# Attention of chunk 3 in 64x64 quarters, narrower P V products in chunks 3 to 7, and the next chunk's transposes moved between the two parts of attention

## The chip, the cores and the metric

One NeuronCore of a Trainium2 chip runs the kernel. The metric is the device time of one execution in microseconds (us); a kernel is run several times and the median is taken. Beside the times there is a profile of one execution. Its engines are PE (TensorE matmuls), PEld (TensorE weight loads), DVE (VectorE), ACT (ScalarE), POOL (GpSimd) and SP (SyncE, here only the queue that issues most of the DMAs). In the profile's shapes, "64*128 64x256" is a matmul with 64 rows and 128 columns of weights whose moving operand has 256 columns. One fp32 matmul instruction of the kernel shows as two matmul records and two weight loads.

## The reference, cut to what matters

The first half is an mLSTM cell over 4 batches, 8 heads, 768 steps and 40 dimensions, the second half a feed-forward layer on its output.

```python
for t in range(S):
    m_new = np.maximum(f_gate[:, :, t] + m, i_gate[:, :, t])
    f_stab = np.exp(f_gate[:, :, t] + m - m_new)
    i_stab = np.exp(i_gate[:, :, t] - m_new)
    m = m_new
    C = f_stab * C + i_stab * einsum('bhd,bhe->bhde', vt, kt)
    n = f_stab * n + i_stab * kt
    h_tilde = einsum('bhde,bhe->bhd', C, qt)
    denom = maximum(abs(sum(n * qt)), 1.0)
    y[:, :, t] = sigmoid(o_gate) * h_tilde / denom
x = y.transpose(0, 2, 1, 3).reshape(3072, 320)
out = maximum(x @ w_in, 0) ** 2 @ w_out      # w_in 320 x 2048, w_out 2048 x 320
```

## The kernel before

**Chunks.** The sequence is cut into chunks of 128 tokens, six per batch, 24 in all, numbered s. Inside a chunk the recurrence is written as attention. With k and q of a chunk transposed (`transposes`, PE, followed by two copies out of PSUM), `scores` forms k q for all pairs of tokens, `weigh` makes the decay weights W (ACT), `mask` and `mask_W` set the pairs to zero in which the key is later than the query token (POOL), and `weighted` multiplies scores by W into P (DVE). P has keys in rows and tokens in columns, so its block of late keys (64 to 127) and early tokens (0 to 63) is all zero. The output of a chunk is P V plus the state C of the chunk before times q; the new state is a decayed C plus k V.

**Three ways of attention.** Chunks 0 to 3 use `attend`: full-height matmuls, `hi` (C q, 4 instructions with 82 columns), `dC` (k V, 4 with 82) and `hp` (P V, 8 with 41). Chunks from `X_SQ` = 4 on use `attend_begin` and `attend_end`: 64x64 quarters of the array, so that four matmuls of different quarters can run beside each other, with the output turned (`numT`). Two quarters that add into the same place of PSUM may not do so at once, so the work is in two parts, with the rows swapped in the second, and between the parts stands a small DVE instruction (L718, one element) that reads the last output of the first part and writes a spare element of kq which the second part reads. In chunks 4 to 7 `values_of_P` (L746) multiplies all 128 columns of P in both parts. In chunks from `ROT` = 8 on the zero block is left out already (the second part has 64 columns).

**Order of the work.** The order on each engine is that in which the code issues it; it is written by hand. The first phase is the loop over u = 0 to 7, where s = 2 + u // 2. In an even u come the scores of chunk s and a part of the first product of the feed-forward layer (`ffn1`); in an odd u come the attention of chunk s, the transposes of chunk s + 1 (L553), the copies out of PSUM (L556, ACT), and another part of `ffn1` (L896 and L907). Between them runs the rounding of the weights (`rounding`): ACT takes the raw words apart (L216, L218), three DVE instructions follow (L227, L231, L232), and POOL joins the result into `w_in` or `w_out` (L236). Each `ffn1` part waits for the pieces of `w_in` that it reads. In u = 3 the attention of chunk 3 stands in the DVE queue behind the rounding of the last pieces of `w_in`.

The second phase starts at chunk 6. `ffn2` (L934) gives the first two chunks' rows of the output; from n = 4 on `ffn1_open` and `ffn1_close` (L1056) and `ffn2_fast` (L980) do the feed-forward layer with fewer products, made from sums of blocks: `sums_of_x` (L1048, L1051, DVE for the first group) needs the normalised rows of chunks 4 and 5, transposed. These rows go through memory: the output of a chunk is stored by SP (`store_num`, L795), loaded turned (`load_num`, L800), normalised on DVE (`normalise_turned`, L812 to L825), stored (`store_rows`, L850), loaded again (`load_rows`, L855) and transposed on DVE in squares (`turn_squares`, L862). SP issues these in program order, each after the landing of the one that it depends on. The first `ffn1_open` multiplies a block X from xT and then a block Y from the sum at L1051.

The state of chunks 1 to 5 is in two tiles `C_old` (by head pairs, two halves) whose flat views are `C_flat`. `decay_old` (POOL) makes the decayed state Cd for the next chunk.

Of the kernel before, what the change touches and what calls it, by code (L numbers as in the profile page):

```python
# [9 lines left out]
F32 = mybir.dt.float32  # L10
# [4 lines left out]
ALU = mybir.AluOpType  # L15
PSUM = bass.MemoryType.PSUM

P = 128
# [11 lines left out]
def kernel(  # L30
# [27 lines left out]
    nc = tc.nc  # L58
    B, H, S, D = q.shape
    BH = B * H  # L60
    NB = S // P
    NT = B * NB
    PR = H // 2
    DP = 64
    D1 = D + 1
# [6 lines left out]
    W = 4 * P  # L72
# [10 lines left out]
    ps_at = ctx.enter_context(tc.tile_pool(name="ps_at", bufs=3, space=PSUM))  # L83
# [236 lines left out]
    st = {}  # L320
# [11 lines left out]


    SQ = 32
    KQ_SQ, X_SQ, ROT = 7, 4, 8
    HALVES = slice(0, DP), slice(DP, 2 * DP)

    def pair_up(s):
# [48 lines left out]
    def kqT(s):  # L387
        t = kqT_b[s % NKT]
        st.setdefault(s, {}).update(kT=t[:, 0], qT=t[:, 1])
        return t  # L390
# [156 lines left out]
    def transposes(s, o=(False, False)):  # L547
        d = st[s]
        kqT(s)
        for i, n in enumerate(("kT", "qT")):  # L550
            tp = bank(o[i])
            for j in range(PR):
                nc.tensor.transpose(  # L553
                    tp[:, j, :], d["kq"][:, i, 2 * j : 2 * j + 2, :].rearrange("p h d -> p (h d)"), ident[:],
                )
            (nc.vector.tensor_copy if s == 1 else nc.scalar.copy)(d[n], tp)  # L556

    def scores(s, o=(False, False)):
        d = st[s]
# [41 lines left out]
            nc.vector.tensor_tensor(t, d["sc"][i], d["W"][:, heads, :] if s < ROT else t, op=ALU.mult)  # L601

    C_old, C_flat = [], []

    def num_tile():
        return old.tile([P, 4 * P], F32, name="num", bufs=1)

    def decay_old(s):
        if s + 1 < NB:
            Cd = st[s]["Cd"] = old.tile([P, PR, 2, D1], F32, name="Cd", bufs=1)  # L610
            if s >= X_SQ:
                st[s]["Cd"] = Cd = Cd[:].rearrange("p j i d -> p (j i d)")[:, : PR * D1].rearrange("p (j d) -> p j d", d=D1)
                for i, rows in enumerate(HALVES):
                    nc.gpsimd.tensor_tensor(
                        Cd[rows], C_old[(s - 1) % 2][rows, :, i, :],
                        st[s]["dec"][rows, i::2].unsqueeze(2).to_broadcast([DP, PR, D1]), op=ALU.mult,
                    )
                return
            nc.gpsimd.tensor_tensor(
                Cd[:].rearrange("p j i d -> p (j i) d"), C_old[(s - 1) % 2].rearrange("p j i d -> p (j i) d"),  # L620
                st[s]["dec"][:].unsqueeze(2).to_broadcast([P, H, D1]), op=ALU.mult,
            )

    def attend(s):
# [48 lines left out]
        if c + 1 < NB:  # L673
# [7 lines left out]
            if s != 1:  # L681
                decay_old(s + 1)

    def scale_q(s):
        if s % NB > 0:
            d = st[s]
            nc.vector.tensor_tensor(d["eA"], d["eA"], d["qT"], op=ALU.mult)

    def decay_C(s):
        if s % NB > 0:  # L690
# [2 lines left out]
                Cd, C_b[(s - 1) % 2][:, : PR * D1].rearrange("p (j d) -> p j d", d=D1),  # L693
                st[s]["eA"][:, :, P - 1 : P].to_broadcast([P, PR, D1]), op=ALU.mult,
            )

    LIVE = [slice(DP * i, DP * i + D) for i in range(2)]

    def state(s):
        return (C_b if s >= NB else C_flat)[s % 2]  # L700
# [1 line left out]
    def attend_begin(s):  # L702

        b, c = divmod(s, NB)
        d = st[s]
        out = d["out"] = [ps_at.tile([P, W], F32, name="numT", tag="at") for _ in range(2)]
        d["numT"] = [t[:, : 2 * P].rearrange("p (c t) -> p c t", t=P) for t in out]
        d["dC"] = [t[:, 2 * P : 2 * P + 2 * D1].rearrange("p (e d) -> p e d", d=D1) for t in out]
        if c > 0:
            values_of_C(s, (0, 1))  # L710
        for i in range(2):
            values_of_P(s, i, (0, 1), False)
        if c + 1 < NB:
            new_C(s, (0, 1), False)
            end, spare = out[1][DP : DP + 1, 2 * P + D1 : 2 * P + D1 + 1], d["kq"][DP : DP + 1, 0, 2, DP - 1 :]
        else:
            end, spare = out[1][DP : DP + 1, P : P + 1], state(s - 1)[0:1, 4 * D1 : 4 * D1 + 1]
        nc.vector.tensor_scalar(spare, end, scalar1=0.0, scalar2=None, op0=ALU.mult)  # L718

    def values_of_C(s, rows, order=(0, 1)):  # L720
        d = st[s]
        C = state(s - 1)
        for e in order:
            for m in order:
                i, j = rows[m], 2 * m + e
                at = (2 * j + i if s == X_SQ else j) * D1
                nc.tensor.matmul(  # L727
                    d["numT"][m][HALVES[e], i, :], lhsT=C[LIVE[i], at : at + DP], rhs=d["eA"][LIVE[i], j, :],
                    start=(i == m), stop=False, skip_group_check=True,
                )  # L730
# [5 lines left out]
    def values_of_P(s, i, rows, second):  # L736
        d = st[s]
        t0 = DP if second and s >= ROT else 0
        for e in range(2):
            for m in range(2):  # L740
                at, keys = slot(s, m, e, i, second), HALVES[rows[m]]
                if s < ROT:
                    rhs = d["P"][i][keys, 2 * m + e, :]
                else:
                    rhs = d["P"][i][keys, e, slice(0, DP) if second else slice(DP, 3 * DP)]
                nc.tensor.matmul(  # L746
                    d["numT"][m][HALVES[e], i, t0:], lhsT=va_w[s % NKQ][keys, at * D1 : at * D1 + DP], rhs=rhs,
                    start=(s % NB == 0 and i == 0 and not second), stop=True, skip_group_check=True,
                )
# [44 lines left out]
    def store_num(s):  # L794
        nc.sync.dma_start(n_d[s], st[s]["tn"].rearrange("p m j r -> p (m j r)"))  # L795
# [31 lines left out]
    def normalise(s):  # L827
        d = st[s]
        num = d["num"]
        if num is not d["hp"]:  # L830
            nc.vector.tensor_tensor(num, num, d["hp"][:], op=ALU.add)
        dm = work.tile([P, H], F32, name="dm")
        nc.vector.tensor_scalar(dm[:], num[:, :, D], scalar1=-2.0, scalar2=2.0, op0=ALU.mult, op1=ALU.max)
        nc.vector.scalar_tensor_tensor(dm[:], in0=num[:, :, D], scalar=2.0, in1=dm[:], op0=ALU.mult, op1=ALU.max)
        nc.vector.reciprocal(dm[:], dm[:])

        x = d["x"] = work.tile([P, 3 * P], F32, name="x_sb")
        x3 = x[:, :DM].rearrange("p (h d) -> p h d", d=D)
        nc.vector.scalar_tensor_tensor(x3, in0=d["og"], scalar=1.0, in1=num[:, :, :D], op0=ALU.add, op1=ALU.mult)
        nc.vector.tensor_tensor(x3, x3, dm[:].unsqueeze(2).to_broadcast([P, H, D]), op=ALU.mult)  # L840
# [323 lines left out]
    load_part(2, 0)  # L1164
    load_part(2, 1)
    idle(12)
    transposes(0)
    idle(4)
    spread_mask(0)
    spread_mask(0)  # L1170
# [9 lines left out]
    eA_turned = turn_gates(A_sb, eA_T, later=True)  # L1180
    weigh(0)
    eA_turned()
    transposes(1, (False, True))
    scores(0)
    spread_mask(1)
    spread_mask(1)
# [28 lines left out]
    turn_rows(0)  # L1215
    idle(2)
    turn_rows(1)
    transposes(2)
    weigh(2, masked=True)
    decay_old(2)  # L1220
    rounding.words()
# [5 lines left out]
    for u in range(8):  # L1227
        s = 2 + u // 2
# [38 lines left out]
        else:  # L1267
# [7 lines left out]
            if u == 5:  # L1275
                half_tanh(4)
                half_tanh(5)
            if s < X_SQ:
                attend(s)
            else:  # L1280
                attend_begin(s)
                attend_end(s)
                store_num(s)
            if u == 3:
                square_half()
            if u != 3:
# [11 lines left out]
                load_A(7)  # L1298
            if u > 4:
                load_num(s)  # L1300
            transposes(s + 1, (True, True))
            rounding.words()
            ffn1(u // 4, u % 4)
            if u != 3:
# [212 lines left out]
```

## Time and profile before

| | |
|---|---|
| median of 3 runs | 486.27 us (486.13 to 487.68) |
| span of the profiled execution | 485.6 us |
| PE busy | 476.8 us (98%), 6229 matmul records and as many weight loads |
| DVE, ACT, POOL busy | 341.1, 243.3, 228.2 us |
| granted TensorE clock | 1.000 over the span |
| DMA share, 50 to 86 us and 132 to 300 us | 0.98 and 0.75 |

The profiled execution's own time is known as its span; what lies around it is inside the 0.7 us by which the median stands above it. PE is busy all the time, so what matters is the time in which PE does nothing or does work that isn't needed, and what PE would wait for if it came earlier. The first phase ends near 86 us and has the densest DMA traffic; from 132 us on the pattern repeats with a period of about 37 us.

### The profile page before, as it was taken

What the parts mean: (1) busy time and instruction counts of PE and PEld (TensorE: products, weight loads), DVE (VectorE), ACT (ScalarE), POOL (GpSimd) and SP (SyncE); (2) the same over time, 40 slices, a digit from 0 to 9 for tenths busy, and PEclk for the clock granted to TensorE, in tenths of its full rate; (3) what the DMA queues carried; (4) which work ended last, traced back from release to release, by engine and by line L of the source; (5) the groups of instructions that cost most, each with busy time, mean ns of one, the idle gap of its engine ahead of it and who ended that gap; (6) DMA issues with size and microseconds to landing.
All of it is one profiled execution on the core that took longest, in us unless ns stands there. A gap on an engine that the chain in (4) does not pass through costs nothing.

```text
span 485.6 us, 15406 instructions
## 1 busy us (share of the span) xinstructions
PE 476.8 (98%) x6229; PEld 445.3 (92%) x6229; DVE 341.1 (70%) x719; ACT 243.3 (50%) x534; POOL 228.2 (47%) x335
## 2 busy tenths in 40 slices
PE   8999999999999999999999999998999999999997
PEld 5886887779999999999999999998999999999997
DVE  7879778788986766767776866765966956635441
ACT  4699797635733722923723932732942741513300
POOL 5464554657598196098097097098084040020000
PEclk9999999999999999999999999999999999999999
DMA  8999997789977767778867757758645613210000
GB/s 181 225 246 266 262 222 206 206 139 205 176 157 192 130 122 205 134 140 185 141 130 195 136 118 203 139 114 208 125 98 155 126 45 84 52 33 2 1 28 27
DMA packets 192695, 69.92 MB, mean 144 GB/s; under 512 B 158128, under 2 KB 181360, under 8 KB 192624
## 3 DMA queue, kind: packets, MB, share of 16 engines
q1 hardware_dynamic: 186400, 58.68, 56.3%
q0 software_dynamic: 6080, 10.16, 9.0%
q8 instruction: 49, 0.80, 0.7%
q14 instruction: 22, 0.18, 0.2%
q10 hardware_dynamic: 144, 0.10, 0.1%
HBM read 55.69 MB, written 18.92 MB: 154 GB/s over the span
## 4 chain that ended last, share of the span: by engine, by line
PE 87%; DVE 6%; ACT 3%; issue 2%; POOL 1%; DMA 1%; DVEq 0%; POOLq 0%
PE h_ps L980 34%; PE h_ps L1056 24%; PE h_ps L1089 6%; PE h_ps L896 4%; PE h_ps L934 4%; PE numT L746 3%; PE numT L727 2%; PE numT L757 1%; PE h_ps L907 1%; PE h_ps L579 1%; PE tp L587 1%; PE tp L553 1%; PE tp L579 1%; PE hp L660 1%; DMA i_sb<-in_i_gate_dram 1%
## 5 line engine op out<-in xcount | busy, mean ns | idle before, releaser
L478 POOL TENSOR_SCALAR_AFFINE_SELECT A_bc<-A_bc 64x512 f32<-64x512 f32 x32 | 24.3, 759 | 88.1 <-ACT kq L496 56.2
L1070 ACT COPY r_sb<-h_ps 128x512 f32<-128x512 f32 x20 | 11.7, 586 | 84.6 <-PE h_ps L1056 84.6
L980 PE MATMUL h_ps<-T,S 128*128 128x160 f32 x352 | 51.7, 300 | 0.5 <-ACT g L1105 0.5
L980 PEld LDWEIGHTS h_ps<-T,S 128*128 128x128 f32 x352 | 48.9, 190 | 1.0 <-ACT g L1105 0.9
L980 PE MATMUL h_ps<-w_out,g 128*128 128x160 f32 x336 | 49.2, 303 | 0.0
L980 PEld LDWEIGHTS h_ps<-w_out,g 128*128 128x128 f32 x336 | 46.1, 190 | 1.3 <-issue 0.7
L996 DVE TENSOR_TENSOR y_sb<-y_sb,h_ps 128x160 f32<-128x160 f32 x44 | 14.0, 319 | 45.6 <-PE h_ps L980 45.4
L1056 PE MATMUL h_ps<-xT,w_in 128*128 128x128 f32 x320 | 43.2, 278 | 0.6 <-issue 0.6
L1056 PE MATMUL h_ps<-lent_t,w_in 128*128 128x128 f32 x320 | 42.3, 275 | 0.0
L1056 PEld LDWEIGHTS h_ps<-xT,w_in 128*128 128x128 f32 x320 | 39.2, 192 | 2.0 <-issue 1.7
L375 POOL DMA_DIRECT2D va<-in_v_dram x64 | 39.2, 623 | 3.0 <-DMA kq_rows<-in_k_dram 2.5
L1089 PE MATMUL h_ps<-xT,w_in 64*64 64x128 f32 x960 | 39.1, 272 | 0.0
L1056 PE MATMUL h_ps<-lent_t 128*128 128x128 f32 x320 | 39.0, 275 | 0.0
L1056 PEld LDWEIGHTS h_ps<-lent_t,w_in 128*128 128x128 f32 x320 | 38.9, 192 | 0.0
L1056 PEld LDWEIGHTS h_ps<-lent_t 128*128 128x128 f32 x320 | 37.3, 192 | 0.0
L509 ACT ACTIVATE A_bc<-A_bc,b_R 128x64 f32<-128x64 f32 (+1 forms) x128 | 35.7, 361 | 2.3 <-POOL A_bc L478 1.9
L1089 PEld LDWEIGHTS h_ps<-xT,w_in 64*64 64x64 f32 x960 | 34.8, 133 | 1.3
L780 DVE STREAM_TRANSPOSE tn<-numT 128x256 f32<-128x256 f32 x36 | 14.1, 428 | 29.1 <-PE numT L727 20.0
L896 PE MATMUL h_ps<-xT,w_in 128*128 128x256 f32 x128 | 29.8, 383 | 0.5 <-POOL w_in L236 0.4
L1048 POOL TENSOR_TENSOR lent_t<-xT 128x128 f32<-128x128 f32 (+1 forms) x18 | 14.6, 829 | 32.7 <-DVE xT L862 32.7
L980 PE MATMUL h_ps<-w_out,g_c 128*128 128x160 f32 x192 | 28.0, 302 | 0.0
L896 PEld LDWEIGHTS h_ps<-xT,w_in 128*128 128x128 f32 x128 | 23.5, 190 | 4.5 <-POOL w_in L236 1.3
(223 smaller groups left out, 1150.1 us busy)
## 6 DMA issues: line engine op xcount, KB each, us to landing
A_bc<-a_slots SPq DMA_DIRECT2D x32, 256.0 KB, 4.5
kq<-num_rows SPq DMA_DIRECT2D x80, 64.0 KB, 2.4
num_rows<-tn SPq DMA_DIRECT2D x18, 256.0 KB, 2.6
raw<-in_moe_w_out_dram SPq DMA_DIRECT2D x7, 640.0 KB, 5.8
kqT<-kq_rows SPq DMA_DIRECT2D x34, 128.0 KB, 3.8
og<-in_o_gate_dram SPq DMA_DIRECT2D x24, 160.0 KB, 5.1
x_rows<-x_sb SPq DMA_DIRECT2D x20, 192.0 KB, 3.6
xT<-x_rows SPq DMA_DIRECT2D x80, 48.0 KB, 3.4
```

The source lines that it names most:

```text
L375: eng.dma_start(dst[HALVES[n], PR * (1 - late_keys) : PR * (2 - late_keys)], src[HALVES[late_keys], PR * m : PR * (m + 1)],)
L478: nc.gpsimd.affine_select(part, part, compare_op=ALU.is_ge, fill=-1e30, base=0, pattern=[[0, PR], [0, 2], [1, DP]], channel_multiplier=-1,)
L509: nc.scalar.activation(A[0][:, x, to], A[0][:, x, to], AF.Exp, bias=b_R[:, b, c, own, x : x + 1],)
L746: nc.tensor.matmul(d["numT"][m][HALVES[e], i, t0:], lhsT=va_w[s % NKQ][keys, at * D1 : at * D1 + DP], rhs=rhs, start=(s % NB == 0 and i == ...
L780: nc.vector.transpose(to[:, 2 * m : 2 * m + 2], d["numT"][m].rearrange("p c t -> p (c t)"))
L896: nc.tensor.matmul(hs[i][:, n, :], lhsT=w_in[:, a, fb * P : (fb + 1) * P], rhs=xT[:, :, a, :], start=(n == 0 and a == 0), stop=False,)
L934: nc.tensor.matmul(st["o_ps"][j], lhsT=st["g2", 0][:, fb, j * P : (j + 1) * P], rhs=w_out[:, fb, :], start=(fb == 0), stop=(fb == NF - 1),)
L980: nc.tensor.matmul(to, lhsT=lhsT[:, p], rhs=rhs[:, p, :], start=(start and p == 0), stop=(p == NPAIR - 1), skip_group_check=True,)
L996: add = lambda to, a, b: nc.vector.tensor_tensor(to, a, b, op=ALU.add)
L1048: sub = lambda to, a, b: eng.tensor_tensor(to, a, b, op=ALU.subtract)
L1056: nc.tensor.matmul(to[:, n, :], lhsT=lhsT[:, 4 * q + n, :], rhs=rhs, start=(start and n == 0), stop=True, skip_group_check=True,)
L1089: nc.tensor.matmul(to[cols, n, :], lhsT=w_in2[rows, 4 * q + n, cols], rhs=rhs, start=(start and n == 0), stop=True, skip_group_check=True,)
```

## The change

Chunk 3 gets an attention of its own in 64x64 quarters (`QUART` = 3): `rows_begin` with 16 instructions for C q, 12 for P V and 8 for k V, each with 41 columns, and `rows_end` with 8 for k V and 12 for P V. It has two parts and a one-element DVE instruction between them, as the later chunks have. The output isn't turned; DVE takes it in two halves. The four blocks of P V per head pair are three, the zero block is not multiplied. The state of chunk 3 is written flat, so chunk 4 reads it flat; Cd of chunk 3 is made by two POOL instructions on 64 partitions in place of one on 128. In chunks 4 to 7 those matmuls of `values_of_P` that read late keys take 64 columns in place of 128. In u = 3, 5 and 7 `transposes(s + 1)` is issued between the two parts of attention, and its copies out of PSUM are issued where they were.

```diff
     SQ = 32
-    KQ_SQ, X_SQ, ROT = 7, 4, 8
+    QUART, KQ_SQ, X_SQ, ROT = 3, 7, 4, 8
...
     def transposes(s, o=(False, False)):
...
-            (nc.vector.tensor_copy if s == 1 else nc.scalar.copy)(d[n], tp)
+            made.append((d[n], tp))
+
+        def copies():
+            for to, tp in made:
+                (nc.vector.tensor_copy if s == 1 else nc.scalar.copy)(to, tp)
+
+        return copies
...
     def decay_old(s):
-            if s >= X_SQ:
+            if s >= QUART:
...
                 for i, rows in enumerate(HALVES):
+                    C = C_old[(s - 1) % 2][rows, :, i, :]
+                    if s > QUART:
+                        C = C_flat[(s - 1) % 2][rows, : PR * D1].rearrange("p (j d) -> p j d", d=D1)
                     nc.gpsimd.tensor_tensor(
-                        Cd[rows], C_old[(s - 1) % 2][rows, :, i, :],
+                        Cd[rows], C,
...
+    def quarter(s, i, half, at, lhsT, rhs):
+        d = st[s]
+        nc.tensor.matmul(
+            d["out"][i][HALVES[half], at : at + D1], lhsT=lhsT, rhs=rhs, start=(i, half) not in d["begun"], stop=True,
+            skip_group_check=True,
+        )
+        d["begun"].add((i, half))
+
+    def rows_of_P(s, swap):
+        for j in range(PR):
+            for keys, toks in ((0, 0), (1, 1), (0, 1)):
+                i = keys ^ swap
+                quarter(
+                    s, i, toks, j * D1, d["P"][i][HALVES[keys], j, HALVES[toks]], d["va"][HALVES[keys], 2 * j + i, :],
+                )
+
+    def rows_of_k(s, swap):
+        for e in (1, 0) if swap else (0, 1):
+            for i in range(2):
+                for m in range(2):
+                    keys, h = HALVES[m ^ swap], 4 * m + 2 * e + i
+                    quarter(s, m, i, 2 * HD + e * D1, d["kq"][keys, 0, h, :], d["vw"][keys, h, :])
+
+    def rows_begin(s):
+        for j in range(PR):
+            for toks in range(2):
+                for i in range(2):
+                    quarter(
+                        s, i, toks, HD + j * D1, d["qT"][LIVE[i], j, HALVES[toks]],
+                        C_old[(s - 1) % 2][LIVE[i], j, i, :],
+                    )
+        rows_of_P(s, 0)
+        rows_of_k(s, 0)
+        end, spare = d["out"][1][DP : DP + 1, 2 * HD + D1 : 2 * HD + D1 + 1], d["kq"][DP : DP + 1, 0, 2, DP - 1 :]
+        nc.vector.tensor_scalar(spare, end, scalar1=0.0, scalar2=None, op0=ALU.mult)
+
+    def rows_end(s):
+        rows_of_k(s, 1)
+        rows_of_P(s, 1)
+        num = d["num"] = num_tile()[:, : H * D1].rearrange("p (h d) -> p h d", d=D1)
+        for i in range(2):
+            nc.vector.tensor_tensor(
+                num[:, i::2, :], view(d["out"][i], HD), eA_T[:, b, c, i::2].unsqueeze(2).to_broadcast([P, PR, D1]),
+                op=ALU.mult,
+            )
+        Cn = C_flat[s % 2][:, :HD].rearrange("p (m x) -> p m x", m=2)
+        for m in range(2):
+            nc.vector.tensor_tensor(
+                Cn[:, m], d["out"][m][:, 2 * HD : 2 * HD + 2 * D1],
+                d["Cd"].rearrange("p (m e) d -> p m (e d)", m=2)[:, m], op=ALU.add,
+            )
+        decay_old(s + 1)
...
     def values_of_P(s, i, rows, second):
                 if s < ROT:
-                    rhs = d["P"][i][keys, 2 * m + e, :]
+                    t0 = DP * rows[m]
+                    rhs = d["P"][i][keys, 2 * m + e, t0:]
...
     def normalise(s):
-        if num is not d["hp"]:
+        if s == QUART:
+            for i in range(2):
+                nc.vector.tensor_tensor(num[:, i::2, :], num[:, i::2, :], d["hp"][i], op=ALU.add)
+        elif num is not d["hp"]:
...
-            if s < X_SQ:
+            if s < QUART:
                 attend(s)
             else:
-                attend_begin(s)
-                attend_end(s)
-                store_num(s)
+                (rows_begin if s < X_SQ else attend_begin)(s)
+                copies = transposes(s + 1, (True, True))
+                (rows_end if s < X_SQ else attend_end)(s)
+                if s >= X_SQ:
+                    store_num(s)
...
-            transposes(s + 1, (True, True))
+            if s < QUART:
+                copies = transposes(s + 1, (True, True))
+            copies()
             rounding.words()
             ffn1(u // 4, u % 4)
```

More of the change, by code (lines that the diff above doesn't have):

```diff
@@ L549, in transposes @@
         kqT(s)
+        made = []
         for i, n in enumerate(("kT", "qT")):
@@ L603 @@
     C_old, C_flat = [], []
+    LIVE = [slice(DP * i, DP * i + D) for i in range(2)]
     def num_tile():
@@ L682, in attend @@
                 decay_old(s + 1)
+    HD = PR * D1
+    def quarter(s, i, half, at, lhsT, rhs):
[6 more added lines that the diff above has]
+    def rows_of_P(s, swap):
+        d = st[s]
+        for j in range(PR):
[4 more added lines that the diff above has]
+                )
@@ new lines, in rows_of_k @@
+    def rows_of_k(s, swap):
+        d = st[s]
+        for e in (1, 0) if swap else (0, 1):
[4 more added lines that the diff above has]
+    def rows_begin(s):
+        d = st[s]
+        d["out"], d["begun"] = [ps_at.tile([P, W], F32, name="numT", tag="at") for _ in range(2)], set()
+        for j in range(PR):
[9 more added lines that the diff above has]
+        nc.vector.tensor_scalar(spare, end, scalar1=0.0, scalar2=None, op0=ALU.mult)
@@ new lines, in rows_end @@
+    def rows_end(s):
+        b, c = divmod(s, NB)
+        d = st[s]
+        rows_of_k(s, 1)
+        rows_of_P(s, 1)
+        view = lambda t, at: t[:, at : at + HD].rearrange("p (j d) -> p j d", d=D1)
+        num = d["num"] = num_tile()[:, : H * D1].rearrange("p (h d) -> p h d", d=D1)
+        d["hp"] = [view(t, 0) for t in d["out"]]
+        for i in range(2):
[10 more added lines that the diff above has]
+        decay_old(s + 1)
@@ L695, in decay_C @@
             )
-    LIVE = [slice(DP * i, DP * i + D) for i in range(2)]
     def state(s):
@@ L725, in values_of_C @@
                 i, j = rows[m], 2 * m + e
-                at = (2 * j + i if s == X_SQ else j) * D1
+                at = j * D1
                 nc.tensor.matmul(
@@ L1166 @@
     idle(12)
-    transposes(0)
+    transposes(0)()
     idle(4)
@@ L1182 @@
     eA_turned()
-    transposes(1, (False, True))
+    transposes(1, (False, True))()
     scores(0)
@@ L1217 @@
     turn_rows(1)
-    transposes(2)
+    transposes(2)()
     weigh(2, masked=True)
```

## The prediction

> **What bounds the kernel now.** I read the page first, then the chain that ended last, then the order in time of each engine around chunks 3 to 7, and at last SP's queue. From the page, the busy times, the shares of the chain and the queue that carries PE's instructions:
>
> ```profile
> PE 476.8 (98%) x6229; PEld 445.3 (92%) x6229; DVE 341.1 (70%) x719; ACT 243.3 (50%) x534; POOL 228.2 (47%) x335
> ...
> PE 87%; DVE 6%; ACT 3%; issue 2%; POOL 1%; DMA 1%; DVEq 0%; POOLq 0%
> ...
> q8 instruction: 49, 0.80, 0.7%
> ```
>
> PE is busy 98% and carries 87% of the chain, so PE work taken out is worth its time if nothing else comes late. PE's order in time around chunks 3 and 4 (start, length, instruction; idle time before it in brackets):
>
> ```profile
> 47.99 1.12 PE L637 MATMUL hi<-Co,kqT 128*128 128x82 f32 x8
> 48.94 1.06 PE L649 MATMUL dC<-vw,kq 128*128 128x82 f32 x8
> 49.84 1.92 PE L660 MATMUL hp<-va,g_c 128*128 128x41 f32 x16
> 51.58 1.07 PE L553 MATMUL tp<-ident,kq 128*128 128x128 f32 x8
> 52.49 3.62 PE L896 MATMUL h_ps<-xT,w_in 128*128 128x256 f32 x16
> ...
> 64.35 0.39 PE L757 MATMUL numT<-vw,kq 64*64 64x41 f32 x16
> 65.02 0.44 PE L757 MATMUL numT<-vw,kq 64*64 64x41 f32 x16 [0.28 <-DVE kq L718]
> 65.28 0.65 PE L746 MATMUL numT<-g_c,va 64*64 64x128 f32 x16
> 65.74 0.40 PE L727 MATMUL numT<-kq,Co 40*64 40x128 f32 x8
> 66.08 1.09 PE L553 MATMUL tp<-ident,kq 128*128 128x128 f32 x8
> ```
>
> Start to start, full-height matmuls of 41 columns (L660) cost 109 ns a record (1.74 us for 16), quarters of 41 columns (L757) 13 to 16 ns (0.26 us for 16). Between the parts of chunk 4 PE waits for the DVE instruction L718. At the same time on DVE and POOL:
>
> ```profile
> 49.64 0.69 DVE L232 SCALAR_TENSOR_TENSOR mag<-raw,mag 128x512 int32<-128x512 int32 x1
> 50.25 0.49 DVE L668 TENSOR_TENSOR num<-hi,eA_T 128x328 f32<-128x328 f32 x1
> 50.48 1.27 POOL L236 TENSOR_TENSOR w_in<-mag,low 128x512 int32<-128x512 int32 x1 [1.16 <-DVE mag L232]
> ```
>
> DVE reaches the attention of chunk 3 at 50.25 only, and the last piece of `w_in` is done at 51.75. Both follow from a DVE queue without a gap since 40.57, which no PE work of this change feeds.
>
> **Chunk 3.** Old: 47.99 to 51.58, 3.59 us. New: 36 instructions, 72 records, before the wait, 20 instructions, 40 records, after it. At 58 ns a round of four (0.20 to 0.26 us for L757's four rounds), with C q in 8 rounds, P V in 8 (three of four quarters used) and k V in 4, the first part takes 1.16 us; the second, 4 and 8 rounds, 0.70. That is 1.73 us of PE work less. The Trainium skill speaks against it: "TensorEngine Tiling (Array Packing)", section "Instruction Overhead", gives each matmul some 60 cycles and advises against tiling a dimension that is small already; at the 25 ns which that estimate makes, 112 records are 2.8 us and 0.8 us less. L757's 13 to 16 ns with 41 columns say otherwise.
>
> Not all of it counts. The first part ends near 49.2, the transposes (0.91 us) near 50.2 with 0.1 us for the change of form on each side (L727 to L553: 0.34 us where its 8 records take 0.22). The one-element instruction takes 0.16 us on DVE and starts at 50.25, behind L232, so PE goes on at 50.46 and ends the second part near 51.25, against 52.49 for the same place. Then `ffn1` issues one matmul and its second waits for POOL's 51.75. Such a wait stands in the trace at 43.70, 0.05 us after the L236 that ends at 43.65, with L907 3.22 us later. So L907 starts at 51.80 + 3.22 = 55.02 against 56.04: **1.02 us** earlier. Without POOL's wait it would be about 1.2. Transposes of chunk 4 need its k and q, issued by SP at 37.94 and 38.38 and landed by 46.2, early enough.
>
> On DVE one short instruction comes new and num, the state and the sum are two halves each (L668's 0.49 becomes two of some 0.3): x of chunk 3 ends near 55.2, not 54.66, while PE reads it near 56.1. The cover is 0.9 us; beyond it the delay would be PE's. POOL's Cd of chunk 3 is two instructions (1.39 us for two such at 53.60, 0.74 for the one at 35.7), in 1.1 us in which POOL is idle. It may hold DVE's L231 beside it 0.3 us longer or let it go 0.3 earlier; I take 0.
>
> **Chunks 4 and 5.** Between the parts PE starts 0.50 us after its last start where a round takes 0.06: 0.45 us lost at 65.02, as much at 78.39. The transposes fill it, and have two changes of form more, 0.1 us each: **0.25 us** each, 0.5 together (0 if the changes cost 0.2, 0.45 if nothing). DVE is idle before L718 there, and the copies out of PSUM stay behind other ACT work.
>
> **The zero blocks.** L746 takes 0.44 us for 16 records, four rounds of 109 ns. In each round two quarters keep 128 columns and two get 64, so the round lasts as long: **0**. The bounds: half of what 64 columns everywhere give (0.26 us for 16 at 131.79), 0.09 us in 8 parts or 0.7 us gained; or widths that run one after the other, as in L579 (16 of 128 columns and 16 of 64 take 0.69 us), 0.23 us in 8 parts or 1.8 us lost.
>
> **The cap.** PE would come to the second phase 1.02 + 0.5 = 1.52 us earlier. What is late next is the way of chunks 4 to 6 through memory. Rows of SP, DVE and PE, in this order:
>
> ```profile
> 92.58 2.06 SPq L855 DMA_DIRECT2D xT<-x_rows  x4
> 94.74 0.40 SPq L795 DMA_DIRECT2D num_rows<-tn  x1
> 96.02 0.38 SPq L850 DMA_DIRECT2D x_rows<-x_sb  x1
> 97.22 1.74 SPq L800 DMA_DIRECT2D kq<-num_rows  x4
> ...
> 102.13 0.17 DVE L812 TENSOR_SCALAR dm<-kq 128x8 f32<-128x8 f32 x1 [0.23 <-DMA kq<-num_rows]
> 105.20 0.28 DVE L1051 TENSOR_TENSOR lent_t<-lent_t,xT 128x128 f32<-128x128 f32 x1
> ...
> 106.80 1.95 PE L1056 MATMUL h_ps<-lent_t 128*128 128x128 f32 x16
> ```
>
> SP issues from 50.41 on with hardly a pause, at a DMA share of 0.98, each row held by the landing before it; L812 waits for a load, and L1051, which the block Y at 106.80 needs, ends at 105.48. None of it moves with PE. So PE gains at most 106.80 - 105.54 = **1.26 us** here, whatever it saved before; the last piece of `w_out` (POOL, done at 102.09, read at 103.76) allows 1.6. If SP's queue does move, 1.5. I take 1.3.
>
> **Stalls of instruction supply.** In the second phase PE stands still, "issue" being a wait that no row explains, at 151.16 (0.59 us) and here:
>
> ```profile
> 335.10 0.21 PE L746 MATMUL numT<-A_bc,va 64*64 64x64 f32 x1 [1.23 <-issue]
> ```
>
> 0.80 MB in 49 packets are 16 KB each, 256 instructions if PE's 12458 records and its semaphore waits fill them, and the instructions that stall are numbers 3266 and 8898 of PE's order: 5632 apart, 22 packets exactly. Both stand at the end of a dense stretch (288 instructions in 3.7 us; there are nine) in which another packet's boundary lies 15 to 35 instructions from the start. The change puts 160 instructions in front of them, so other stretches are hit: by the count only the one at 109.58, 21 from its start. One stall of 1.2 to 2 us for 1.82 us: **0.3 us** gained, between 1.8 gained and 1.8 lost. The Trainium skill ("Runtime: NRT & Kernel Launch", section "Instruction fetch mechanics") has PE's instructions refilled in 16 KiB blocks, mostly hidden. The trace shows the blocks, but not these two as hidden; by that page the term would be 0.
>
> **The sum.** The profiled execution's span of 485.6 less 1.3 and 0.3 is 484.0; the median stands 0.67 above that span, so 486.27 - 1.6 = 484.6 or 484.7; I say **484.6**.
>
> **Rivals.** (1) *SP's queue moves along and the widths help*: 1.52 + 0.4 of zero blocks, and a stall less: 483.2 to 484.2. For it: DMAs free up when their readers come earlier. Against: the continuous SP rows. (2) *Mixed widths run one after the other*: six parts before the cap cost 1.4 us, so 1.52 shrinks to 0.1, two parts behind it cost 0.5: 485.5 to 486.7. (3) *Part of the gain only*: chunk 3's quarters wait longer for DVE, or the DMA way comes later by half a microsecond: 485.0 to 485.8. (4) *Slower, by instruction supply*: the new dense stretches of chunk 3 in the time of full DMA, and chunk 7's, starve as at 335.10, 1.23 us each. It decides from the point at which new stalls outweigh 1.3 us and the old ones stay: three new ones give 486.27 - 1.3 + 3.7 = 488.7. For it: 224 instructions where 64 were; against: nine such stretches have two stalls.
>
> **How the numbers follow.** A measurement of this kernel can tell about 0.3%, 1.46 us, so faster is below 484.81. Forecast 0.45 (484.1 to 485.0), rival 1 0.2, rival 2 0.12, rival 3 0.17, rival 4 0.06. Faster: 0.7 of the forecast and all of rival 1, 0.52; slower 0.06 and a little of rival 2, 0.07; the same 0.41. The range, 483.2 to 486.2, leaves out rival 4, the upper part of rival 2 and a little of rival 1.
>
> **What would show it.** Right: L896 after chunk 3 with its second matmul held by POOL at 51.8; no idle time before the second parts of chunks 4 and 5; L746 still 0.44 us; L1056's block Y held by DVE near 105.5, and an "issue" gap near 111 in place of those at 151 and 335. Wrong: L746 at 0.26 or at 0.67 us; a block Y that starts before 105; rows of chunk 3 over 2 us; "issue" gaps between 48 and 70.

## The result, and the profile after

The changed kernel takes 485.15 us (median of 20 runs, 483.78 to 487.64), the kernel before on the same chip 486.58 us (20 runs, 485.26 to 489.69). The ratio is 0.9963, 95% interval 0.9947 to 0.9980: 1.4 us faster by the medians and 1.8 by the ratio, at the edge of the 0.3% that the prediction took as what can be told from no change. The prediction was 484.6 us, with 483.2 to 486.2 as its range.

The page of the changed kernel: busy times, shares of the chain, the queue of PE's instructions.

```profile
PE 476.5 (98%) x6307; PEld 443.9 (92%) x6309; DVE 342.4 (71%) x722; ACT 243.2 (50%) x534; POOL 224.9 (46%) x336
...
q8 instruction: 50, 0.82, 0.7%
...
PE 83%; DMA 5%; DVE 4%; ACT 3%; SPq 2%; issue 1%; POOL 1%; DVEq 0%; POOLq 0%; ACTq 0%
```

PE is still what the time goes by, and there is one packet of instructions more. The profiled execution took 486.42 us, its span is 484.7: 1.7 us lie around the span, as in the other runs whose time and span are both known. The profiled execution of before, with a span of 485.6, must then have taken some 487.3 us, above its median and not below it.

PE's order in time around chunks 3 and 4 (start, length, instruction; idle time before it in brackets; L983 was L907, L972 was L896, L830 was L757):

```profile
49.24 1.09 PE L554 MATMUL tp<-ident,kq 128*128 128x128 f32 x8
50.99 0.44 PE L699 MATMUL numT<-vw,kq 64*64 64x41 f32 x16 [0.66 <-DVE kq L735]
...
51.83 3.72 PE L972 MATMUL h_ps<-xT,w_in 128*128 128x256 f32 x16
55.48 1.13 PE L983 MATMUL h_ps<-xT,w_in 64*128 64x256 f32 x8
...
64.11 1.09 PE L554 MATMUL tp<-ident,kq 128*128 128x128 f32 x8
65.14 0.44 PE L830 MATMUL numT<-vw,kq 64*64 64x41 f32 x16
```

Chunk 3 starts at 47.93. Its first part lasts 1.31 us to the transposes, its second 0.84 us. Between transposes and second part PE is idle for 0.66 us: it waits for the one-element DVE instruction L735. In chunk 4 the second part starts right behind the transposes, without idle time. The same time on DVE and POOL:

```profile
48.45 1.11 DVE L227 TENSOR_SCALAR mag<-mag 128x512 f32<-128x512 f32 x1 [0.59 <-ACT mag L216]
...
50.06 0.69 DVE L232 SCALAR_TENSOR_TENSOR mag<-raw,mag 128x512 int32<-128x512 int32 x1
50.78 0.16 DVE L735 TENSOR_SCALAR kq<-numT 1x1 f32<-1x1 f32 x1
...
50.89 1.27 POOL L236 TENSOR_TENSOR w_in<-mag,low 128x512 int32<-128x512 int32 x1 [1.62 <-DVE mag L232]
```

DVE, without a pause there before, now waits 0.59 us for ACT, and L735 ends at 50.94 in place of the 50.41 that was forecast. The way to block Y (SP's queue, DVE, PE):

```profile
97.99 1.74 SPq L873 DMA_DIRECT2D kq<-num_rows  x4
...
105.67 0.29 DVE L1127 TENSOR_TENSOR lent_t<-lent_t,xT 128x128 f32<-128x128 f32 x1
...
106.11 2.02 PE L1132 MATMUL h_ps<-lent_t 128*128 128x128 f32 x16
```

Y comes 0.69 us earlier than before, block X 0.86 us earlier; the 0.17 us between the two are a wait for the sum, which here ends at 105.96, later than before. And the places where PE stands still for "issue":

```profile
113.02 0.45 PE L799 MATMUL numT<-kq,C 40*64 40x128 f32 x7 [0.54 <-issue]
...
262.68 0.27 PE L1132 MATMUL h_ps<-xT,w_in 128*128 128x128 f32 x1 [0.74 <-issue]
```

The stalls at 151 and 335 us are gone; these two are new.

Since the first 45 us differ by some 0.2 us from run to run, the experiments are compared from the start of `ffn1`'s 64-row products (L907 or L983) in u = 2, near 46.9 us. The table has what each trace shows from there, in us:

| kernel | to the same products in u = 3 | from u = 4's to u = 5's | from u = 6's to u = 7's | to ffn2's first product | to block Y |
|---|---|---|---|---|---|
| before | 9.11 | 7.97 | 7.52 | 39.11 | 59.88 |
| changed | 8.62 | 7.82 | 7.37 | 38.29 | 59.24 |
| r1, changed again | 8.61 | 7.82 | 7.37 | 38.28 | 59.04 |
| q1, quarters only | 8.21 | 7.97 | 7.52 | 38.20 | 58.97 |
| t1, transposes only | 9.11 | 7.82 | 7.37 | 38.81 | 59.57 |
| w1, full width | 8.19 | 7.82 | 7.37 | 37.88 | 58.65 |
| b1, early instruction | 8.08 | 7.82 | 7.36 | 37.76 | 58.52 |
| n1, no P V in 4, 5 | 8.20 | 6.94 | 6.50 | 36.14 | 57.64 |

The times come from three sets of runs, each with the kernel before beside it: at 486.40 us for q1, s1, s2 and s3, at 486.45 for t1, w1, p1 and c1, at 486.73 for r1, b1, b2 and n1.

### The profile page after: what moved, and what is told of

Read it like the earlier page. It is cut to its first block, busy times and chain, and to the rows that moved or that the text cites. A ratio compares the mean times of both kernels' runs of the same rounds, so it can differ in the third digit from the quotient of the medians.

```text
span 484.7 us, 15567 instructions
## 1 busy us (share of the span) xinstructions
PE 476.5 (98%) x6307; PEld 443.9 (92%) x6309; DVE 342.4 (71%) x722; ACT 243.2 (50%) x534; POOL 224.9 (46%) x336
## 4 chain that ended last, share of the span: by engine, by line
PE 83%; DMA 5%; DVE 4%; ACT 3%; SPq 2%; issue 1%; POOL 1%; DVEq 0%; POOLq 0%; ACTq 0%
PE h_ps L1056 32%; PE h_ps L1132 24%; PE h_ps L1165 7%; PE h_ps L972 4%; PE h_ps L1010 4%; PE numT L819 3%; PE numT L799 2%; ACT g_c L515 1%; PE numT L830 1%; DMA num_rows<-tn 1%; DMA kqT<-kq_rows 1%; PE h_ps L983 1%; PE tp L594 1%; PE h_ps L586 1%; PE tp L586 1%
## 5 line engine op out<-in xcount | busy, mean ns | idle before, releaser
L478 POOL TENSOR_SCALAR_AFFINE_SELECT A_bc<-A_bc 64x512 f32<-64x512 f32 x32 | 23.1, 721 | 88.1 <-ACT kq L496 59.3
L1056 PEld LDWEIGHTS h_ps<-w_out,g 128*128 128x128 f32 x336 | 46.1, 190 | 1.3 <-issue 0.9
L1124 POOL TENSOR_TENSOR lent_t<-xT 128x128 f32<-128x128 f32 (+1 forms) x18 | 15.6, 887 | 32.7 <-DVE xT L938 32.7
L972 PE MATMUL h_ps<-xT,w_in 128*128 128x256 f32 x128 | 30.1, 386 | 0.5 <-POOL w_in L236 0.4
L972 PEld LDWEIGHTS h_ps<-xT,w_in 128*128 128x128 f32 x128 | 23.4, 190 | 5.0 <-POOL w_in L236 1.3
```

The costliest lines, as they stand in the source:

```text
L478: nc.gpsimd.affine_select(part, part, compare_op=ALU.is_ge, fill=-1e30, base=0, pattern=[[0, PR], [0, 2], [1, DP]], channel_multiplier=-1,)
L972: nc.tensor.matmul(hs[i][:, n, :], lhsT=w_in[:, a, fb * P : (fb + 1) * P], rhs=xT[:, :, a, :], start=(n == 0 and a == 0), stop=False,)
L1056: nc.tensor.matmul(to, lhsT=lhsT[:, p], rhs=rhs[:, p, :], start=(start and p == 0), stop=(p == NPAIR - 1), skip_group_check=True,)
L1124: sub = lambda to, a, b: eng.tensor_tensor(to, a, b, op=ALU.subtract)
```

## Experiments: the parts of the change

**q1: chunk 3 in quarters alone.** Only chunk 3 has the new attention, with the transposes inside.

```diff
-                copies = transposes(s + 1, (True, True))
+                if s < X_SQ:
+                    copies = transposes(s + 1, (True, True))
...
-                    t0 = DP * rows[m]
-                    rhs = d["P"][i][keys, 2 * m + e, t0:]
+                    rhs = d["P"][i][keys, 2 * m + e, :]
```

> One part of the change alone: chunk 3 in quarters with the transposes of chunk 4 between its parts; chunks 4 and 5 have their transposes behind the second part as before, and P V reads all 128 columns in chunks 4 to 7. Theory: the rate of a round is 58 ns, so the first part takes 1.16 us and 0.15 for the change of form, the second 0.70 and 0.15; what counts is decided by the last piece of w_in (POOL, 51.7 to 52.2 us): ffn1's 64-row products of chunk 3 start 3.3 us after that piece, at 55.0 to 55.5, in place of 56.04, so 0.5 to 1.0 us are gained there; in chunks 4 and 5 the idle time of about 0.45 us before the second parts is back, and phase one ends 0.5 to 1.0 us earlier than before, where the full change has 0.9 to 1.4. Rival (the quarters bring nothing by themselves, and what the full change gains comes from the transposes): 56.0 and an end of phase one as before.

Measured: 0.90 us in chunk 3 (9.11 to 8.21), nothing in chunks 4 and 5, Y 0.91 us earlier; 485.28 us, ratio 0.9953 (0.9928 to 0.9978). The quarters bring most of the gain, and more here than in the first trace of the full change. The rival falls.

**t1: the transposes alone.** In the kernel before, `transposes(s + 1)` of u = 5 and 7 moves between `attend_begin` and `attend_end`, its copies stay.

```diff
                 attend_begin(s)
+                copies = transposes(s + 1, (True, True))
                 attend_end(s)
                 store_num(s)
...
-            transposes(s + 1, (True, True))
+            copies()
```

> The kernel before, with one part of the change: in u = 5 and 7 the next chunk's transposes stand between the two parts of attention; chunk 3 and P V as before. Times are taken from the start of ffn1's 64-row products in u = 2 (46.9 us in both traces), so that what comes before them doesn't count. Theory (0.45 us of idle time filled, two more changes of form at 0.1 us each): 0.25 us gained in chunk 4 and as much in chunk 5; ffn2's first product, 39.12 us after that point in the kernel before, comes at 38.6 to 38.8, and block Y, 59.88 us in the kernel before, at 59.3 to 59.5. Rival (the changes of form cost as much as the gap): 39.1 and 59.9. The median is 0 to 1 us below the kernel before.

Measured: 0.15 us in each chunk in place of 0.25; ffn2's first product at 38.81 and Y at 59.57, just outside what was expected. PE in time:

```profile
64.63 1.09 PE L554 MATMUL tp<-ident,kq 128*128 128x128 f32 x8
65.65 0.44 PE L764 MATMUL numT<-vw,kq 64*64 64x41 f32 x16
```

The idle time is filled, but from transposes to second part it is 1.02 us, where transposes followed by `ffn1` took 0.93, and the first two products of `ffn1` now start 0.32 us apart instead of 0.22. The two more changes of form cost 0.15 us each. The time, 486.41 us (ratio 1.0, 0.9976 to 1.0024), can't show 0.3 us.

**w1: full width.** The changed kernel with the second part of q1's diff: P V of chunks 4 to 7 reads all 128 columns.

> The changed kernel, but P V of chunks 4 to 7 reads all 128 columns in both parts, zero blocks too. Theory (a round lasts as long as its widest quarter): P V parts of 16 records keep 0.43 to 0.46 us; ffn2's first product and block Y stand as in the changed kernel, 38.0 to 38.3 and 58.8 to 59.3 us after ffn1's 64-row products of u = 2; median within 0.5 us of the changed kernel's. Rival 1 (64 columns save a part of each round): the parts take 0.1 us longer than in the changed kernel, 0.4 us by block Y. Rival 2 (mixed widths run one after the other): the parts are 0.1 to 0.2 us shorter than in the changed kernel.

Measured: chunks 4 and 5 as in the changed kernel, 7.82 and 7.37 us. Chunk 6 stands between ffn2's first product and block X: 19.87 us here and before, 19.87 to 19.89 in the traces with the narrow products (n1, which lacks other work, apart). The zero blocks cost nothing; both rivals fall. 484.33 us (ratio 0.9961, 0.9940 to 0.9981), no slower than the full change. Chunk 3 took 8.19 us here, 0.43 less than in the first trace of the change, although its code is the same; so ffn2's first product (37.88) and Y (58.65) came ahead of what was expected. DVE and POOL show where that comes from:

```profile
47.80 0.42 DVE L227 TENSOR_SCALAR mag<-mag 128x512 f32<-128x512 f32 x1
...
50.38 0.16 DVE L735 TENSOR_SCALAR kq<-numT 1x1 f32<-1x1 f32 x1
...
48.02 1.32 POOL L236 TENSOR_TENSOR w_in<-lent_t 128x512 int32<-128x512 int32 x1 [1.62 <-DVE lent_t L232]
```

**r1: the changed kernel again.**

> The changed kernel once more, with nothing changed, for a second profile and more times. Theory (chunk 3's gain is set by the DVE instruction between its parts, which is queued behind a rounding that ACT feeds from a DMA; ffn1's 64-row products start 4.54 us after its end in four traces): from the start of these products in u = 2 to those in u = 3 it takes 8.2 to 8.6 us, the sooner the earlier ACT's last pass over w_in starts; any stall without a cause behind 100 us stands 190 to 195 instructions past a multiple of 256, its length another than in the first trace. Median within 0.5 us of 485.15. Rival (the 8.62 us of the first trace are the kernel's own): 8.6 again.

Measured: 8.61 us, 485.58 us (ratio 0.9969, 0.9945 to 0.9993), one "issue" gap of 0.20 us at 260.35, 190 instructions past a multiple of 256. DVE and POOL:

```profile
48.18 1.37 DVE L227 TENSOR_SCALAR mag<-mag 128x512 f32<-128x512 f32 x1 [0.33 <-ACT mag L216]
...
50.77 0.16 DVE L735 TENSOR_SCALAR kq<-numT 1x1 f32<-1x1 f32 x1
...
47.99 1.28 POOL L236 TENSOR_TENSOR w_in<-lent_t 128x512 int32<-128x512 int32 x1 [1.62 <-DVE lent_t L232]
```

In the first trace ACT had waited 0.59 us for a DMA of `w_in` at 40.39; here it was 0.26 us earlier, and chunk 3 no faster, so "the sooner, the earlier ACT" is not the rule. It is a step. POOL's L236 of the piece before starts at 47.9 to 48.2 us in all these traces and lasts 1.3 to 1.5 us. Where DVE's L227 starts ahead of it (47.63, 47.80, 47.98, 47.99 us in q1, w1, s3, n1) it takes 0.42 us, and L231 behind it is the one that lasts 1.4 us, until POOL is done. Where L227 comes after POOL's start (48.45 and 48.18 in the two traces of the change), L227 itself lasts until then, and L231 follows with another 0.43. L735 ends near 50.4 to 50.75 in the first case, at 50.93 to 50.94 in the second. In seven traces u = 3's 64-row products start 4.54 or 4.55 us after L735's end. The two cases are read off these traces; no run changed the order of the two starts and nothing else.

## Experiments: what holds chunk 3

**p1: the last piece of w_in read late.** In all `ffn1` parts of phase one the products that read the first block of rows (a = 0) come first.

```diff
-        for i in range(2):
-            for n in range(2):
-                fb = 4 * pp + 2 * n + i
-                for a in range(2):
+        for a in range(2):
+            for i in range(2):
+                for n in range(2):
+                    fb = 4 * pp + 2 * n + i
```

> The changed kernel, with the eight 128-row products of each ffn1 part of phase one in another order: the four that read the first block of w_in's rows come first, the four that read the second block last, so that the piece of w_in that POOL finishes last is read 1.75 us later. Times from the start of ffn1's 64-row products in u = 1 (38.7 us). Theory (POOL's last piece binds chunk 3's gain, and SP's and DVE's chain binds block Y): the wait of 0.40 us at 43.65 goes; after chunk 3 ffn1 doesn't wait for POOL; ffn2's first product, 46.45 us after that point in the changed kernel's trace and 47.34 before, comes at 45.7 to 46.1; but block Y, 67.40 in the changed kernel and 68.10 before, comes at 66.8 to 67.1 only, with idle time or a DVE sum ahead of it. The median is 0 to 0.6 us below the changed kernel's. Rival (SP's chain moves along with PE): block Y comes as much earlier as ffn2, at 66.6 or below. Rival 2 (POOL binds nothing): 46.4.

Measured: the wait at 43.65 went and `ffn1` doesn't wait for POOL after chunk 3, but none of the gain came. Chunk 3's second part is held until 51.08, and `ffn1` takes the same 3.65 us from its start to the 64-row products although it reads the last piece late.

```profile
51.08 0.44 PE L699 MATMUL numT<-vw,kq 64*64 64x41 f32 x16 [1.08 <-DVE kq L735]
...
73.21 2.86 PE L972 MATMUL h_ps<-xT,w_in 128*128 128x256 f32 x12 [0.20 <-ACT g L996]
```

What PE gains early it waits for at L735 (1.08 us of idle time). The second row shows a new loss: the order takes its second PSUM bank 0.9 us sooner, and ACT hasn't emptied it. ffn2's first product came 47.29 us after u = 1's 64-row products, where 45.7 to 46.1 was expected, and Y at 68.06 (66.8 to 67.1). 485.06 us, ratio 0.9967 (0.9948 to 0.9987). With L735 where it is, POOL's piece does not bind chunk 3, and the first two starts of `ffn1` 0.32 us apart are there here too: they are the change of form.

**b1: the DVE instruction one place earlier.** `rows_begin` is issued ahead of the last of the three rounding instructions on DVE, with POOL's order unchanged (`first` issues L227 and L231, `second` L232 and L236); in `ffn1` of u = 3 alone, each bank has its a = 0 products first.

```diff
-                rounding.join()
-                mask_W(4)
-                values(4)
+                rounding.join(first=True)
...
+            if u == 3:
+                rows_begin(s)
+                rounding.join(second=True)
+                mask_W(4)
+                values(4)
```

> The changed kernel with the one-element DVE instruction of chunk 3 one place earlier in DVE's queue, ahead of the last instruction of the rounding (0.69 us) in place of behind it; and in ffn1 of u = 3 the two products of a bank that read the first block of w_in's rows come first, since that block's last piece is now done 0.16 us later. Theory (the DVE instruction is what holds chunk 3): the second part starts at about 50.2 us right behind the transposes with no idle time, and from ffn1's 64-row products of u = 2 to those of u = 3 it takes 7.8 to 8.0 us, where the changed kernel took 8.2 to 8.6; block Y comes 58.3 to 58.9 after the former. Median 0.2 to 0.6 us below the changed kernel's. Rival (POOL's piece of w_in binds): 8.2 to 8.6 as before, with ffn1 waiting for POOL.

```profile
49.79 0.16 DVE L738 TENSOR_SCALAR kq<-numT 1x1 f32<-1x1 f32 x1
...
50.25 0.44 PE L702 MATMUL numT<-vw,kq 64*64 64x41 f32 x16
...
51.09 3.92 PE L974 MATMUL h_ps<-xT,w_in 128*128 128x256 f32 x16
```

The hold is gone, the second part follows the transposes, and `ffn1` starts 0.74 us earlier than in the first trace. It then takes 3.85 us to its 64-row products in place of 3.65: now POOL's piece, 0.16 us later, does bind, for 0.2 us. So 8.08 us (7.8 to 8.0 was expected), Y at 58.52 with the sum ready 0.20 us ahead. The median, 485.5 us (ratio 0.9965, 0.9943 to 0.9986), is that of the changed kernel beside it (485.58): 0.5 us of PE time does not show in it.

**b2: the same order in all parts.**

```diff
-            for n, a in ((0, 0), (1, 0), (0, 1), (1, 1)) if (g, pp) == (0, 3) else ((0, 0), (0, 1), (1, 0), (1, 1)):
+            for n, a in ((0, 0), (1, 0), (0, 1), (1, 1)):
```

> The kernel with the early one-element instruction, and the order of products of its ffn1 part used in all eight parts of ffn1 in phase one. Theory: the wait of 0.40 us for POOL at 43.65 goes as well, or shrinks to 0.1; the 64-row products of u = 2 come 7.8 to 7.95 us after those of u = 1, where it was 8.16 to 8.24; chunk 3 then waits up to 0.3 us for DVE, so that u = 3's come 15.9 to 16.1 after u = 1's (16.4 to 16.8 in the changed kernel, 17.34 before). PSUM banks are taken in the same order as before, so no new wait for ACT, unlike the kernel with the late piece. Median 0.2 to 0.8 us below the changed kernel's. Rival (DVE's own chain sets chunk 3 in any case): no further gain over the kernel with the early one-element instruction.

Measured: the wait at 43.65 went, but u = 2's products came 8.09 us after u = 1's, and u = 3's 16.42 after, where b1 has 16.26: PE waits 0.17 us for POOL at 51.99. The rival is right, DVE and POOL set this stretch. 485.59 us (ratio 0.9972, 0.9948 to 0.9995).

## Experiments: the cap at block Y

**c1: sums first.** p1's kernel, with the squares and sums of chunk 5 ahead of chunk 6's normalisation on DVE.

```diff
+            if n == 2:
+                turn_squares(5)
+                sums_of_x(2)
             do(normalise_turned, s)
             do(store_rows, s)
             if n == 2:
                 pair_up(9)
-                turn_squares(5)
-                sums_of_x(2)
```

> The kernel with the late piece, and on DVE the squares and sums of chunk 5 (which block Y reads) ahead of the normalisation of chunk 6, which takes 2.1 us there. Theory (Y's cap is DVE's place in line behind chunk 6 and the landing of chunk 5's rows): DVE's sum for Y ends 0.5 to 2 us earlier, block Y follows block X without a wait, at 65.9 to 66.5 us after ffn1's 64-row products of u = 1; the median is 0.3 to 0.9 us below that of the kernel with the late piece. Rival (the landing of the rows alone sets the cap): Y stays at 66.8 to 67.1.

Inconclusive: the sum for Y ended at 104.25, 2.42 us ahead of need, but p1's order had put PE itself back (Y at 68.35 us after u = 1's products). 484.9 us (ratio 0.9962, 0.9938 to 0.9986), not to be told from p1's 485.06.

**n1: less work ahead of Y.**

```diff
         for i in range(2):
-            values_of_P(s, i, (0, 1), False)
+            if s not in (4, 5):
+                values_of_P(s, i, (0, 1), False)
```

and the same in `attend_end`.

> The changed kernel without P V of chunks 4 and 5: 32 matmul instructions, 64 records in 4 parts of 0.44 us, aren't issued, and their share of the output is missing. It takes 1.7 us of PE work out ahead of block Y. Theory of the cap as the prediction has it (SP's chain doesn't move with PE, so that block Y can't come before about 105.5 us): Y at 58.5 to 59.0 us after ffn1's 64-row products of u = 2, with 0.5 to 1.5 us of idle time before it for a DVE sum. Rival (SP's chain moves along with PE, as the trace with full-width P V suggests, where the sum was done 1.1 us ahead of need): ffn2's first product 36.2 to 36.6 and Y 57.0 to 57.5, with less than 0.2 us of idle time. The median is then 1.2 to 1.9 us below the changed kernel's; under the cap 0 to 0.6 below.

```profile
101.42 1.91 PEld L1012 LDWEIGHTS h_ps<-w_out,g 128*128 128x128 f32 x8 [0.61 <-POOL w_out L236]
...
104.30 0.28 DVE L1129 TENSOR_TENSOR lent_t<-lent_t,xT 128x128 f32<-128x128 f32 x1
...
104.73 1.02 PE L1134 MATMUL h_ps<-lent_t 128*128 128x128 f32 x7
```

Y came 57.64 us after the reference point, 0.9 us before the cap's lower end and 0.1 after the rival's upper one, and waited 0.16 us for the sum. 484.13 us, ratio 0.9942 (0.9920 to 0.9964), 1.45 us below the changed kernel beside it. The cap of the prediction, 1.26 us, does not stand. But not all of the work taken out is gained: beside w1, whose chunk 3 took as long, ffn2's first product comes 1.74 us earlier and Y only 1.01. Of the 0.73 us lost between them, 0.16 is the wait for the sum, and a part is a wait for the last piece of `w_out`, for which a weight load stood 0.61 us (first row); the prediction had named that piece as the next limit, at 1.6 us. The sum's end isn't a fixed time: 105.26 to 105.49 us in three traces of before's attention in chunk 3, 103.9 to 106.0 with the quarters. That SP's chain moves along with PE isn't shown either: the sum ended 57.49 us after the reference point in n1 and 57.47 in w1, where no work is missing.

## Experiments: the supply of instructions

In three kernels, s1 from the kernel before, s2 and s3 from the changed one, idle matmuls at the start are cut into narrow ones, so that every later instruction moves on by 160, 18 or 64 places in PE's order: in s1 all 12 and the next 4 into six each, in s2 9 of them into two, in s3 8 into five.

```diff
-    idle(12)
+    idle(12, 12, 6)
```

> The kernel before, with 160 more TensorE instructions at its start and nothing else: 16 of the idle matmuls before the first product are cut into 6 narrow ones each. In the two traces PE's stalls without a cause in the profile stand at instructions 3266 and 8898 (before) and 2238 and 6846 (after): all four 190 to 194 past a multiple of 256. Theory (blocks of 256 instructions are fetched one ahead, and PE stands where it runs through a block in less than about 4 us): the stalls at 151 and 335 us go, and stalls of 0.4 to 1.1 us come near 113 and 262 us, as in the changed kernel; the median is 0 to 1 us below the kernel before. Rival (the stalls belong to the work and the DMA traffic at those places): they stay at 151 and 335 us with 0.6 and 1.2 us, and the time is the same within 0.3 us.

> The changed kernel with 18 more TensorE instructions at its start (9 of the idle matmuls in two narrow halves each), nothing else. Theory of the blocks: this is a bad place for their boundaries, worked out from the changed kernel's trace with 4.0 to 4.4 us for a block: stalls near 112 and 260 us, 1.0 to 1.5 us each, 2.0 to 2.9 us together; the median lies 0.5 to 1.2 us above the changed kernel's, about 486. Rival (the boundaries mean little): stalls as in the changed kernel's trace, 0.5 and 0.7 us, and its median within 0.3 us.

> The changed kernel with 64 more TensorE instructions at its start (8 of the idle matmuls in five narrow parts each), nothing else. Theory of the blocks: this is a good place for their boundaries: stalls of 0.2 to 0.7 us near 260 and 334 us, 0.5 to 1.3 together, none near 113; the median lies 0.3 to 1.0 us below the changed kernel's and 1.0 to 1.7 below the one with 18 more. Rival (the boundaries mean little): the changed kernel's median within 0.3 us.

Measured in s1: the gaps at 151 and 335 us are gone, with nothing changed but the count; none came at 113 or 262, where they were expected. (t1, with the count of before, has both gaps too; none of the twelve traces with another count has one there.) 485.7 us, ratio 0.9983 (0.9961 to 1.0006). In s2: 1.03 us at 113.05 and 0.58 at 264.94, 1.6 us together where 2.0 to 2.9 was expected, and a wait of 2.06 us for ACT at 203.40 that has another cause (before shows 0.46 us at that place); 485.52 us (ratio 0.9974, 0.9949 to 0.9999). In s3, the good place by the theory:

```profile
112.65 0.38 PE L830 MATMUL numT<-vw,kq 64*64 64x41 f32 x12 [1.30 <-issue]
...
136.59 0.68 PE L1056 MATMUL h_ps<-w_out,g 128*128 128x160 f32 x3 [0.55 <-issue]
```

with 486.05 us (ratio 0.9978, 0.9950 to 1.0006). Here stalls of 0.2 to 0.7 us were expected near 260 and 334 us and none near 113, so the theory that forecasts places and lengths from the time of a block fails, and s2 and s3 don't differ as expected. What holds is the count: all "issue" gaps behind 100 us, 14 in eight traces, stand 190 to 195 places past a multiple of 256, counted over matmuls, weight loads and semaphore instructions. So a stall stands where a block of 256 ends; the block's other boundary lies 256 places ahead of it. Why the length varies is in the records of the instruction queue's packets. At twelve of the 14 gaps PE goes on 2.2 to 2.6 us after the start of a packet; in the other two, after 2.9 and 3.0 us, the packet itself took 1.4 and 1.5 us in place of 0.9 to 1.1. In twelve of the 14 PE had run through the block in 3.2 to 3.9 us, in s3's two in 5.3 and 5.8. Nine traces have the boundary of the block that ends near 113 us at the same instruction, and run through it in 2.9 to 3.5 us: in three the packet started 1.41 to 1.59 us after PE had passed the boundary, and PE stood for 0.54 to 0.89 us; in six it started 0.38 to 1.00 us after, and there is no gap. In s3, where that boundary lies elsewhere, it started some 4 us after. What delays a packet was not tried.

## Why the prediction was right, point by point

- **Chunk 3, 1.02 us.** The PE work was priced right: 58 ns a round, 1.15 us from the first to the last record of the first part, 0.68 in the second, so some 16 ns a record. A change of form took about 0.15 us, not 0.1, so that the two parts took 2.15 us with these changes and 1.83 without, on both sides of the 2 us named as a sign of being wrong. The 25 ns, an estimate worked out from the Trainium skill ("TensorEngine Tiling (Array Packing)", section "Instruction Overhead"), don't hold for 64x64 quarters of 41 columns. The hold by the one-element instruction was foreseen, with PE going on at 50.46; in q1 it was 50.44, in the first trace of the change 50.99. Where it failed is the step after the hold: not POOL's piece but L735 ends last, `ffn1` does not wait for POOL (p1), and L735 comes at two times. The term is 0.90 to 0.92 us where DVE's L227 gets ahead of POOL's L236 (q1, w1; 0.77 in s3), and 0.50 where not (both traces of the change). That 1.02 came near 0.9 is luck in so far as it was counted from POOL's end.
- **Chunks 4 and 5, 0.25 us each.** Mis-sized: 0.15 us each (t1), since a change of form costs 0.15 us.
- **Zero blocks, 0.** Right to 0.02 us (w1).
- **The cap, 1.26 us.** Wrong: in n1 Y comes 2.24 us earlier than before. The sum's 105.48 us was one execution's, not a bound. Rival 1 was nearer in that Y can come earlier, but its reason, that the chain follows PE, isn't shown. In the first trace the sum did hold Y, by 0.17 us, at 105.96. The wrong cap cost the forecast little, because without a cap PE has only 0.92 + 0.31 = 1.23 us to bring (w1: Y 1.23 us earlier), and 0.8 in the first trace.
- **Instruction supply, 0.3 us.** Right in that 160 instructions move the stalls, and in the place near 111; not in that only one comes, and not in reading two gaps as the kernel's own. The gaps sum to 1.82 us in the trace of before, and to 1.28 and 0.20 in the two of the changed kernel. From Y to the start of its last matmul PE took 375.34 us before and 375.14 changed, where executions with no gap or hardly one took 372.7 to 373.3 (s1, q1, w1, p1, c1, r1): 1.9 to 2.6 us are lost in either trace, more than the gaps alone (before also waits 0.46 us for ACT at 202), and nearly none in r1, the changed kernel again. The Trainium skill ("Runtime: NRT & Kernel Launch", section "Instruction fetch mechanics") has the refill mostly hidden: true of nearly all 50 blocks, and at times untrue where 256 instructions take 3.2 to 3.9 us (in s3 5.3 and 5.8).
- **The sum.** The medians fall by 1.43 us, forecast 1.6. To block Y the rows account for 0.64 and 0.84 in the two traces of the changed kernel, and for 1.23 in w1. The rest is within what the stalls make of a set of runs, and it stays open how much of it is theirs: s1, the kernel before with 160 places more and no other change, has a median 0.7 us lower, with an interval that takes in no change. So the number 484.6 came near partly by luck: the 1.3 us taken for the rows were too high by 0.5 to 0.7 us in those two traces, and the medians fell by nearly the forecast amount all the same. The medians can't tell the parts apart (ratios of 0.9953 for q1, 0.9961 for w1, 0.9963 for the whole); which part brings what is shown by the traces alone. That the median stood 0.67 us above the span was a comparison of two quantities: the profiled execution's own time was about 487.3.

No kernel with the whole computation is shown to be faster than the changed one.

## What to carry to other kernels

A wait put down to one engine in a trace can hide a second that ends within tenths of a microsecond; follow the instruction that releases PE through its own queue, and look at which neighbour it must get ahead of. Before an end time on a memory chain is used as a cap, see in a second execution whether it is fixed. When gains of half a microsecond are at stake, count in places along the trace from a common point, since stalls of instruction supply can move the whole time by more: they sum to nothing in some of these executions (q1, w1, s1) and to 1.8 us in others (before, s3).

## What the runs showed of the hardware

- A DVE instruction of 0.42 us (L227) that starts while POOL's L236 runs ends 0.3 us after it, and so lasts 1.11 and 1.37 us in the two traces of the change; the next one is short again. The Trainium skill ("SBUF — State Buffer", section "SBUF: two separate sides") has an exclusive lock for a pair of ports that GpSimd shares with some of DVE's instructions, and these rows agree with it. That 0.2 us in the order of two starts goes with 0.4 us of PE's time was not expected.
- PE's instructions come in blocks of 256, and PE can stand idle for 0.2 to 1.3 us at the end of one, depending on when the next packet starts. Twelve of 14 such stalls follow a block that took 3.2 to 3.9 us; other traces run through blocks as short without a stall.
- Where PE goes from quarters to full height or back, some 0.15 us go by. In t1 the first transpose starts 0.16 us after the last quarter, where rounds start 0.06 apart, and the second 0.16 us after the first in place of 0.11; the first quarter after them starts 0.20 us after the last transpose. When `ffn1` follows quarters, its second record comes 0.32 us after its first in place of 0.22.
